# Attention and a gated MLP on one core: the scale of V from a reduction on GpSimd and powers of two on VectorE, in place of a transpose and spreading products on TensorE

## The chip, the core and the metric

The kernel runs on one core of a Trainium2 chip. A core has five engines, each with its own queue of instructions that it works through in order: TensorE (PE, matrix products), VectorE (DVE), ScalarE (ACT), GpSimd (POOL) and SyncE (SP, which issues the transfers here). They wait for each other through semaphores. The time is device microseconds of one execution; a kernel's figure is the median of several runs. One more execution of each kernel is recorded instruction by instruction; from it come the profile's page and the answers of the trace.

## The reference

Sliding-window attention with a linear bias, followed by a gated MLP that mixes along the sequence. B = 8 batches, H = 8 heads, S = 576 positions, D = 64, and d_model = 512, d_ff = 1024. All in 32-bit floats:

```python
scores = scale * np.matmul(q, k.transpose(0, 1, 3, 2))
mask = (rel >= 0) & (rel < window)                    # window = 128
scores = np.where(mask, scores + bias[None], -1e9)
attn = softmax(scores)
x = np.matmul(attn, v)                                # heads side by side: (B, S, 512)
h = np.maximum(x @ w_in, 0.0)
u, v = h[..., :512], h[..., 512:]
v_n = (v - mean(v)) / np.sqrt(var(v) + 1e-6)
v_s = np.einsum('ts,bsd->btd', w_spatial, v_n) + b_spatial[None, :, None]
return (u * v_s) @ w_out
```

## The kernel before

**Precision.** Every factor of a product is kept as two parts, a rounded one and the rest, and a product is made of three passes. In the attention of most pairs the two parts are 16-bit floats. For these, V has to be brought into the range of a 16-bit float first: it is multiplied with a power of two (`am[:, 5:6]`), split into `vh` and `vl`, and the result is multiplied with the inverse (`am[:, 6:7]`, which also takes out the factor 4096 of the probabilities).

**The work.** Heads are worked in pairs, `p` = 0 to 3, so there are 32 pairs of batch and heads. The first five (batch 0, and pair 0 of batch 1) go through `raw_tile`, which needs no scale. The other 27 go through `attention`: scores on PE (L520), bias, mask and minimum on VectorE (L531), exponentials and their sums on ScalarE (L537), the probabilities split into two 16-bit parts `pq` (L557 on ScalarE, L562 on VectorE), transposed by two transfers of SyncE into `pt` (L568), and multiplied with `vh` and `vl` on PE (L624). L633 and L637 scale the result back and split it into `xt`.

**The scale of V (L572 to L601),** once for each of the 27 pairs. ScalarE sums |V| along the free dimension (L579), which gives each of the 128 partitions one number, `am[:, 0:1]`. PE transposes this column into one row (L583), in a bank of PSUM that it takes from the ring `x` of two banks, the ring that the products L624 use as well. VectorE takes the maximum of the row and keeps it between two powers (L587, L588), in 16 bits. Two products of one column (L593) spread it back over 128 partitions, times 2^-12 and times 2^-13/4096 from the constant `ones`. VectorE keeps the exponents alone (L599) and turns the first into its inverse by an exclusive or (L600). Then V is scaled into `vh` (L604 on VectorE or L607 on ScalarE) and `vl` (L611).

**The gated part, `gated(b)`,** for each batch 29 units on PE, each into one of two banks `m`. First five v units, one for each block of positions (L689, and L711 for the last block of 64, which comes second): product, relu on ScalarE (L271), and the layer norm: statistics (L650 to L655, VectorE), 1/sqrt by a `pow` on GpSimd (L659), normalisation (L663, VectorE), then the split into `vn` (a copy by L267, and L700). The buffer `vt` of a block is one of two. Then come u units (L741, relu by L271 on ScalarE or L272 on VectorE), spatial units (L762, which need all five blocks of `vn`) and output units (L788): "uuuuusususs...", so five u units stand ahead of the first spatial one. GpSimd has little to do beside `pow`: constants at the start (L226 to L248, L386, L387), and two clearings of a part of `pq` ahead of the first scaled pair (L491).

**The order.** Nothing is ordered by hand. Each operation is added to a `Plan` with an engine (or a choice of two), a weight in ns, a due time, and what it reads and writes. `Plan.order` walks through time: whatever is ready, by its inputs and its ring of buffers, goes to its engine as soon as that is free, the earliest due time first, and holds the engine for its weight. The order that comes out is each engine's queue; on the chip the times are the chip's own and the order stays. The weights of the steps above: 95 for L583, 190 for L593, 400 for L587 and L588, 150 for L599 and L600, 550 for L659.

Of the kernel before, what the change touches and what calls it, by code (L numbers as in the profile page):

```python
# [9 lines left out]
F32 = mybir.dt.float32  # L10
F32R = mybir.dt.float32r
BF16 = mybir.dt.bfloat16
F16 = mybir.dt.float16
I32 = mybir.dt.int32
U32 = mybir.dt.uint32
AF = mybir.ActivationFunctionType
ALU = mybir.AluOpType
AX = mybir.AxisListType
# [120 lines left out]
def attn_gmlp_kernel(ctx, tc, qk, v, w_in, w_spT, b_sp, w_out, outT):  # L139
# [3 lines left out]
    nc = tc.nc  # L143
    B, H, D, _, S = qk.shape
    P = 2 * D
# [8 lines left out]
    PSC = 4096.0  # L154
    VORDER = (0, 4, 1, 2, 3)

    SWITCH = 190
# [12 lines left out]
    work = ctx.enter_context(tc.tile_pool(name="work", bufs=2))  # L170
    ps = ctx.enter_context(tc.tile_pool(name="ps", bufs=1, space=PSUM))
    ctx.enter_context(tc.manual_schedule())
    plan = Plan()

    def fixed(shape, dtype, name):
        t = const.tile(shape, dtype, name=name)
        return Buf(lambda: t)

    def dve(n, fast=False):
        return 75 + n / (1.92 if fast else 0.96)  # L180
# [13 lines left out]

    nhalf = fixed([P, 1], F32, "nhalf")
    ident = fixed([P, P], F32, "ident")
    ones = fixed([1, 2 * P], BF16, "ones")
    tabs = [fixed([P, 2 * P], BF16, f"tab{h}") for h in range(H)]
    win = fixed([P, NC_, 2, DF], F32R, "win")
    wout = fixed([P, ND, 2, DM], F32R, "wout")  # L200
# [10 lines left out]
    rstat = fixed([P, 8, 8], F32, "rstat")  # L211
# [12 lines left out]
    def constants():  # L224
        def f():
            nc.gpsimd.iota(relf(), [[-1, 2 * P]], base=P, channel_multiplier=1, allow_small_or_imprecise_dtypes=True)  # L226
        plan.add("POOL", 400, 0, f, (), [(relf, 0)])

        def f():
            nc.vector.memset(maskt(), 0.0)  # L230
        plan.add("DVE", dve(256), 0, f, (), [(maskt, 0)])

        def f():
            nc.gpsimd.affine_select(maskt(), maskt(), [[-1, 2 * P]], ALU.is_ge, MASKED, base=P, channel_multiplier=1)
            nc.gpsimd.affine_select(maskt(), maskt(), [[1, 2 * P]], ALU.is_ge, MASKED, base=-1, channel_multiplier=-1)
        plan.add("POOL", 800, 1, f, [(maskt, 0)], [(maskt, 0)])

        def f():
            nc.vector.memset(ident(), 1.0)
            nc.vector.memset(ones()[:, :P], 2.0 ** -12)  # L240
            nc.vector.memset(ones()[:, P:], 2.0 ** -13 / PSC)
            nc.vector.memset(nhalf(), -0.5)
            nc.vector.memset(rstat(), 1.0)
        plan.add("DVE", dve(400), 500, f, (), [(ident, 0), (ones, 0), (nhalf, 0)] + [(rstat, k) for k in range(8)])

        def f():
            nc.gpsimd.affine_select(ident(), ident(), [[-1, P]], ALU.is_ge, 0.0, base=0, channel_multiplier=1)
            nc.gpsimd.affine_select(ident(), ident(), [[1, P]], ALU.is_ge, 0.0, base=0, channel_multiplier=-1)  # L248
        plan.add("POOL", 600, 500, f, [(ident, 0)], [(ident, 0)])

        def f():
            nc.vector.tensor_scalar(minus(), ident(), -1.0, None, ALU.mult)
        plan.add("DVE", 150, 501, f, [(ident, 0)], [(minus, 0)])
        for j in range(2):
            def f(j=j):
                nc.vector.memset(stat[j](), 1.0)
            plan.add("DVE", dve(64), 600, f, (), [(stat[j], x) for x in range(99)])
        for h in range(H):
            def f(h=h):
                slope = 2.0 ** (-8.0 * (h + 1) / H)  # L260
                nc.vector.scalar_tensor_tensor(tabs[h](), relf(), -8.0 * slope, maskt(), ALU.mult, ALU.add)
            plan.add("DVE", dve(256), 1000 + h * 4000, f, [(relf, 0), (maskt, 0)], [(tabs[h], 0)])
# [237 lines left out]
    def attention(b, p):  # L500
# [11 lines left out]
        for g, banks in enumerate(PIECES):  # L512
            sc = [[plan.buf(ps, "s", 4, [P, 2, 2 * P], F32) for _ in range(2)] for _ in banks]
            span = [(k, i, t, min(P, S - t * P), max(0, (t - 1) * P), min(S, (t + 1) * P)) for k, ts_ in enumerate(banks) for i, t in enumerate(ts_)]

            def f(sc=sc, span=span):
                for k, i, t, m, k0, k1 in span:
                    for j in range(2):
                        rows = slice(j * D, (j + 1) * D)
                        nc.tensor.matmul(sc[k][j]()[:m, i, :k1 - k0], raw()[rows, 0, t * P:t * P + m], raw()[rows, 1, k0:k1],  # L520
                                         start=True, stop=True)
            plan.add("PE", SWITCH + pe(*[4 * (x[5] - x[4]) for x in span]), due - 5000 + g * 3000, f, RAWS,
                     [(sc[k][j], i) for k, i, *_ in span for j in range(2)])
            for k, i, t, m, k0, k1 in span:
                for j in range(2):
                    h, n, c0 = 2 * p + j, k1 - k0, P if t == 0 else 0
                    pt = lambda j=j, m=m, t=t, n=n: prob[j]()[:m, OFF[t]:OFF[t] + n]
                    d = due - 4500 + t * 700 + j * 200

                    def f(sc=sc[k][j], pt=pt, i=i, j=j, h=h, t=t, m=m, n=n, c0=c0):  # L530
                        nc.vector.tensor_tensor_reduce(pt(), sc()[:m, i, :n], tabs[h]()[:m, c0:c0 + n], -0.125, 3e38,  # L531
                                                       ALU.add, ALU.min, st()[:m, NM, j, t:t + 1])
                    cols = parts(prob[j], OFF[t], OFF[t] + n)
                    plan.add("DVE", dve(n), d, f, [(sc[k][j], i), (tabs[h], 0)], cols + [(st, (NM, j, t))])

                    def f(pt=pt, j=j, t=t, m=m):
                        nc.scalar.activation(pt(), pt(), AF.Exp, bias=st()[:m, NM, j, t:t + 1], scale=-1.0,  # L537
                                             accum_out=st()[:m, SM, j, t:t + 1])
                    plan.add("ACT", act(n, 2), d, f, cols + [(st, (NM, j, t))], cols + [(st, (SM, j, t))])
        pts = []  # L540
        for j in range(2):
            d = due + j * 1500
# [28 lines left out]

        vh, vl = (plan.buf(work, tag, 2, [P, NQ, P], F16) for tag in ("vh", "vl"))  # L572
        am = plan.buf(work, "am", 2, [P, 8], F32)
        one = plan.buf(work, "one", 2, [1, 2], BF16)
        mp = plan.buf(ps, "x", 2, [P, 512], F32)
        d = due - 3000

        def f():
# [1 line left out]
        plan.add("ACT", act(NQ * P, 1), d, f, VRS, [(vl, 0), (am, 0)])  # L580

        def f():
            nc.tensor.transpose(mp()[0:1, 0:P], am()[:, 0:1], ident())  # L583
        plan.add("PE", SWITCH // 2, d + 1, f, [(am, 0), (ident, 0)], [(mp, 0)])

        def f():
            nc.vector.tensor_reduce(one()[:, 0:1], mp()[0:1, 0:P], AX.X, ALU.max)  # L587
            nc.vector.tensor_scalar(one()[:, 0:1], one()[:, 0:1], 2.0 ** -98, 2.0 ** 126, ALU.max, ALU.min)  # L588
        plan.add("DVE", 400, d + 2, f, [(mp, 0)], [(one, 0)])

        def f():
            for k in range(2):
                nc.tensor.matmul(mp()[:, P + k:P + k + 1], ones()[:, k * P:(k + 1) * P], one()[:, 0:1], start=True, stop=True,  # L593
                                 skip_group_check=True)
        plan.add("PE", SWITCH, d + 3, f, [(one, 0), (ones, 0)], [(mp, 1)])

        def f():
            bits = 0x7F800000
            nc.vector.tensor_scalar(am()[:, 5:7].bitcast(I32), mp()[:, P:P + 2].bitcast(I32), bits, None, ALU.bitwise_and)  # L599
            nc.vector.tensor_scalar(am()[:, 5:6].bitcast(I32), am()[:, 5:6].bitcast(I32), bits, None, ALU.bitwise_xor)  # L600
        plan.add("DVE", 150, d + 4, f, [(mp, 1)], [(am, 1)])  # L601

        def fv():
            nc.vector.tensor_scalar(vh(), vr(), am()[:, 5:6], None, ALU.mult)  # L604
# [61 lines left out]
    def gated(b, xt, first=lambda t: None):  # L666
# [140 lines left out]
        for i, kind in enumerate(UORDER):  # L807
# [3 lines left out]
            {"u": u_unit, "s": sp_unit, "o": o_unit}[kind](*todo[kind].pop(0))  # L811

    constants()
    for c in range(NC_):
        win_weights(1, c, -30000 + 1000 * c, win_load(1, c, -30000 + 1000 * c, f"vn{c}", 1))
# [17 lines left out]
    for b in range(1, B):  # L833
        xt = []
        for p in range(NP):
            if b == 1 and (b, p) not in RAW and (b, p - 1) in RAW:
                clear()
            xt.append(attention(b, p))
        gated(b, xt)
# [33 lines left out]
```

## Time and profile before

| | us |
|---|---|
| median of 3 runs | 648.48 (648.08 to 651.25) |
| profiled execution, whole | 648.05 |
| its span in the trace | 646.3 |
| mean granted clock of TensorE | 0.992 |

Three timed runs and one profiled execution; the profiled one is 0.4 us below the median. Of the trace these groups belong to the scale of V (27 pairs):

| line, engine | count | busy, us | mean, ns |
|---|---|---|---|
| L579 ACT, sums of absolute values | 27 | 19.8 | 734 |
| L583 PE, transpose | 27 | 7.3 | 272 |
| L587 DVE, maximum | 27 | 7.4 | 273 |
| L593 PE, spreading | 54 | 5.3 | 165 |
| L599 DVE, exponents | 27 | 4.1 | 154 |
| L600 DVE, inverse | 27 | 4.2 | 154 |

A busy time counts the instruction's own duration, also where PE's pipeline lets neighbours overlap. A row of a group or of a timeline ends, where the engine was idle ahead of it, with how long and with what ended the idle time. "issue" is idle time without a wait that the profile shows. A time of a timeline is counted from the start of the span. Where an engine's name has a q behind it (POOLq), the row is of its sequencer, not of its arithmetic.

### The profile page before, as it was taken

The numbers are of one execution on the slowest core, as the hardware profiler recorded it, in microseconds if no ns is written. First come the engines' busy times: TensorE is split into PE (matmuls) and PEld (weight loads), VectorE is DVE, ScalarE is ACT, GpSimd is POOL, SyncE is SP. The second block draws the span as 40 slices with busy tenths as digits, with TensorE's granted clock in tenths as the row PEclk, the third lists the DMA queues.
The fourth block names the chain that finished last, engine by engine and source line by source line (L and its number), as shares of the span: only waits on it lengthen the run. The fifth ranks groups of instructions, "written<-read, shape, count | busy, mean of one in ns | idle before, by whom it ended". The sixth has DMA issues, their size and how long they took to land.

```text
span 646.3 us, 14141 instructions
## 1 busy us (share of the span) xinstructions
PE 619.0 (96%) x5037; PEld 529.8 (82%) x5037; DVE 524.2 (81%) x1897; ACT 430.9 (67%) x1322; POOL 29.6 (5%) x53
## 2 busy tenths in 40 slices
PE   4879999999999999999999999999999999999997
PEld 2445688778899879988898979988898978988997
DVE  6999898999887979887887979887887979873632
ACT  4698675989585848686686848676686857662211
POOL 1000010000200010000100010000100010000100
PEclk9998799999999999999999999999999999999999
DMA  7903013799156863778165753858166751733001
GB/s 264 329 20 130 19 62 119 169 209 202 55 132 133 190 107 93 155 155 184 40 143 127 191 112 89 154 152 188 32 154 125 193 113 10 132 79 76 2 20 55
DMA packets 149291, 79.34 MB, mean 123 GB/s; under 512 B 128610, under 2 KB 139874, under 8 KB 149220
## 3 DMA queue, kind: packets, MB, share of 16 engines
q1 hardware_dynamic: 149220, 78.44, 51.8%
q8 instruction: 39, 0.64, 0.4%
q14 instruction: 32, 0.26, 0.1%
HBM read 37.13 MB, written 9.44 MB: 72 GB/s over the span
## 4 chain that ended last, share of the span: by engine, by line
PE 79%; DVE 17%; issue 1%; DMA 1%; ACT 1%; SPq 1%; ACTq 0%; DVEq 0%
PE m L762 16%; PE m L741 16%; PE m L788 14%; PE m L689 13%; PE s L520 8%; PE x L624 6%; DVE pq L562 4%; PE m L711 2%; DVE prob L436 2%; DVE prob L531 2%; DVE gs L298 1%; DMA pt<-in_qk_dram 1%; DVE prob L450 1%; DVE u L770 1%; DVE o L267 1%
## 5 line engine op out<-in xcount | busy, mean ns | idle before, releaser
L537 ACT ACTIVATE prob<-prob,stat 128x128 f32<-128x128 f32 (+1 forms) x270 | 125.4, 466 | 13.6 <-DVE stat L531 12.4
L762 PE MATMUL m<-wsp,vn 128*128 128x288 f32 x768 | 124.3, 299 | 0.7 <-DVE u L770 0.7
L788 PE MATMUL m<-gs,wout 128*128 128x288 f32 x768 | 113.5, 301 | 0.3 <-DVE gs L776 0.2
L762 PEld LDWEIGHTS m<-wsp,vn 128*128 128x128 f32 x768 | 107.5, 188 | 6.7 <-issue 1.9
L557 ACT ACTIVATE pq<-prob,stat 128x128 f16<-128x128 f32 x270 | 103.1, 464 | 12.7 <-ACT prob L537 10.2
L741 PE MATMUL m<-xt,win 128*128 128x288 f32 x768 | 111.6, 298 | 0.0
L788 PEld LDWEIGHTS m<-gs,wout 128*128 128x128 f32 x768 | 103.3, 188 | 7.2 <-issue 1.7
L562 DVE SCALAR_TENSOR_TENSOR pq<-prob,stat,pq 128x128 f16<-128x128 f32 x270 | 104.0, 437 | 4.3 <-ACT pq L557 3.7
L741 PEld LDWEIGHTS m<-xt,win 128*128 128x128 f32 x768 | 103.9, 188 | 4.1 <-issue 2.3
L689 PE MATMUL m<-win,xt 128*128 128x512 f32 x384 | 93.5, 396 | 1.7 <-DVE o L267 1.7
L531 DVE CUSTOM_DVE_ANT_0 prob<-s,tab 128x128 f32<-128x128 f32 (+1 forms) x270 | 89.2, 376 | 2.6 <-PE s L520 2.1
L689 PEld LDWEIGHTS m<-win,xt 128*128 128x128 f32 x384 | 71.5, 189 | 18.2 <-DVE o L267 2.8
L520 PE MATMUL s<-qkraw 64*128 64x256 f32 (+2 forms) x540 | 66.5, 360 | 1.5 <-DVE stat L531 1.3
L770 DVE TENSOR_TENSOR u<-m,u 128x288 f32<-128x288 f32 x64 | 28.9, 451 | 34.2 <-PE m L762 34.2
L520 PEld LDWEIGHTS s<-qkraw 64*128 64x128 f32 (+1 forms) x540 | 42.0, 175 | 16.2 <-issue 9.0
L659 POOL TENSOR_TENSOR st<-st,nhalf 128x1 f32<-128x1 f32 (+1 forms) x40 | 25.6, 640 | 560.4 <-DVE st L655 548.0
L537 ACT ACTIVATION_READ_ACCUMULATOR prob<-prob,stat 128x1 f32 x270 | 50.6, 187 | 0.0
L267 ACT COPY o<-m 128x288 f32<-128x288 f32 x37 | 14.6, 395 | 46.2 <-PE m L788 45.9
L624 PE MATMUL x<-pt,vh 128*64 128x256 f16 (+6 forms) x756 | 41.7, 229 | 0.0
L271 ACT ACTIVATE vt<-m 128x512 f32<-128x512 f32 x31 | 18.5, 598 | 33.0 <-DVE st L654 16.1
L637 DVE SCALAR_TENSOR_TENSOR xt<-x,am,xt 128x288 fp32r<-128x288 f32 x54 | 26.2, 507 | 17.1 <-ACT xt L633 17.0
L624 PEld LDWEIGHTS <-vh 128*64 128x64 f16 x756 | 31.7, 110 | 5.8 <-issue 3.5
(132 smaller groups left out, 820.7 us busy)
## 6 DMA issues: line engine op xcount, KB each, us to landing
qkraw<-in_qk_dram SPq DMA_DIRECT2D x28, 576.0 KB, 3.9
out_dram<-o SPq DMA_DIRECT2D x64, 144.0 KB, 2.0
vraw<-in_v_dram SPq DMA_DIRECT2D x28, 320.0 KB, 2.9
vn<-in_w_in_dram SPq DMA_DIRECT2D x6, 512.0 KB, 7.1
pt<-in_w_out_dram SPq DMA_DIRECT2D x4, 512.0 KB, 4.5
gs<-in_w_spT_dram SPq DMA_DIRECT2D x4, 288.0 KB, 5.0
xt<-in_w_in_dram SPq DMA_DIRECT2D x2, 512.0 KB, 6.8
qkraw<-in_qk_dram SPq DMA_DIRECT2D x3, 320.0 KB, 8.3
```

The lines of the kernel that those rows point to most:

```text
L520: nc.tensor.matmul(sc[k][j]()[:m, i, :k1 - k0], raw()[rows, 0, t * P:t * P + m], raw()[rows, 1, k0:k1], start=True, stop=True)
L531: nc.vector.tensor_tensor_reduce(pt(), sc()[:m, i, :n], tabs[h]()[:m, c0:c0 + n], -0.125, 3e38, ALU.add, ALU.min, st()[:m, NM, j, t:t + 1])
L537: nc.scalar.activation(pt(), pt(), AF.Exp, bias=st()[:m, NM, j, t:t + 1], scale=-1.0, accum_out=st()[:m, SM, j, t:t + 1])
L557: nc.scalar.activation(pq[j]()[:m, 0, cs], prob[j]()[:m, cs], AF.Copy, scale=st()[:m, RC, j, t:t + 1])
L562: nc.vector.scalar_tensor_tensor(pq[j]()[:m, 1, cs], prob[j]()[:m, cs], st()[:m, RC, j, t:t + 1], pq[j]()[:m, 0, cs], ALU.mult, ALU.subtract)
L624: nc.tensor.matmul(xp()[j * D:(j + 1) * D, x0:x0 + n], l()[:, kt, j * D:(j + 1) * D], rhs[:, o:o + n], start=j not in seen, stop=False, sk ...
L637: nc.vector.scalar_tensor_tensor(xt()[:, S + R + hf * HS:S + R + (hf + 1) * HS], xp()[:, :HS], am()[:, 6:7], xt()[:, qs].bitcast(F32), ALU ...
L689: nc.tensor.matmul(pt(), xt[c]()[:, X0[a] + t * P:X0[a] + (t + 1) * P], win()[:, c, w, DH:DF], start=(n == 0), stop=(n == 3 * NC_ - 1))
L741: nc.tensor.matmul(pt()[:, :HS], win()[:, c, w, d * P:(d + 1) * P], xt[c]()[:, X0[a] + hf * HS:X0[a] + (hf + 1) * HS], start=(n == 0), sto ...
L762: nc.tensor.matmul(pt()[:, :HS], l, r, start=(n == 0), stop=(n == len(ops) - 1))
L770: nc.vector.tensor_tensor(u(), pt()[:, :HS], u(), ALU.mult)
L788: nc.tensor.matmul(pt()[:, :HS], wout()[:, d, w, e * P:(e + 1) * P], gs[d]()[:, a, :], start=(n == 0), stop=(n == 3 * ND - 1))
```

## The change

The column `am[:, 0:1]` no longer goes to PE. GpSimd takes the maximum over the 128 partitions and gives it to all of them (`partition_all_reduce`, weight 4000 in the plan). VectorE then limits it, keeps the exponent, multiplies it with the two powers of two, now a constant of 128 partitions by two columns (`powers`), and inverts the first: four operations. `one`, the bank `mp` of the ring `x` and the constant `ones` go. The maximum is no longer rounded to 16 bits on its way; only its exponent is used, as before.

```diff
-    ones = fixed([1, 2 * P], BF16, "ones")
+    powers = fixed([P, 2], F32, "powers")
...
-            nc.vector.memset(ones()[:, :P], 2.0 ** -12)
-            nc.vector.memset(ones()[:, P:], 2.0 ** -13 / PSC)
+            nc.vector.memset(powers()[:, 0:1], 2.0 ** -12)
+            nc.vector.memset(powers()[:, 1:2], 2.0 ** -13 / PSC)
...
-        one = plan.buf(work, "one", 2, [1, 2], BF16)
-        mp = plan.buf(ps, "x", 2, [P, 512], F32)
...
         def f():
-            nc.tensor.transpose(mp()[0:1, 0:P], am()[:, 0:1], ident())
-        plan.add("PE", SWITCH // 2, d + 1, f, [(am, 0), (ident, 0)], [(mp, 0)])
-
-        def f():
-            nc.vector.tensor_reduce(one()[:, 0:1], mp()[0:1, 0:P], AX.X, ALU.max)
-            nc.vector.tensor_scalar(one()[:, 0:1], one()[:, 0:1], 2.0 ** -98, 2.0 ** 126, ALU.max, ALU.min)
-        plan.add("DVE", 400, d + 2, f, [(mp, 0)], [(one, 0)])
-
-        def f():
-            for k in range(2):
-                nc.tensor.matmul(mp()[:, P + k:P + k + 1], ones()[:, k * P:(k + 1) * P], one()[:, 0:1], start=True, stop=True,
-                                 skip_group_check=True)
-        plan.add("PE", SWITCH, d + 3, f, [(one, 0), (ones, 0)], [(mp, 1)])
+            nc.gpsimd.partition_all_reduce(am()[:, 1:2], am()[:, 0:1], P, bass.bass_isa.ReduceOp.max)
+        plan.add("POOL", 4000, d + 1, f, [(am, 0)], [(am, 2)])
 
         def f():
             bits = 0x7F800000
-            nc.vector.tensor_scalar(am()[:, 5:7].bitcast(I32), mp()[:, P:P + 2].bitcast(I32), bits, None, ALU.bitwise_and)
+            nc.vector.tensor_scalar(am()[:, 2:3], am()[:, 1:2], 2.0 ** -98, 2.0 ** 126, ALU.max, ALU.min)
+            nc.vector.tensor_scalar(am()[:, 2:3].bitcast(I32), am()[:, 2:3].bitcast(I32), bits, None, ALU.bitwise_and)
+            nc.vector.tensor_scalar(am()[:, 5:7], powers(), am()[:, 2:3], None, ALU.mult)
             nc.vector.tensor_scalar(am()[:, 5:6].bitcast(I32), am()[:, 5:6].bitcast(I32), bits, None, ALU.bitwise_xor)
-        plan.add("DVE", 150, d + 4, f, [(mp, 1)], [(am, 1)])
+        plan.add("DVE", 400, d + 4, f, [(am, 2), (powers, 0)], [(am, 1)])
```

More of the change, by code (lines that the diff above doesn't have):

```diff
@@ L239, in f @@
             nc.vector.memset(ident(), 1.0)
-            nc.vector.memset(ones()[:, :P], 2.0 ** -12)
-            nc.vector.memset(ones()[:, P:], 2.0 ** -13 / PSC)
+            nc.vector.memset(powers()[:, 0:1], 2.0 ** -12)
+            nc.vector.memset(powers()[:, 1:2], 2.0 ** -13 / PSC)
             nc.vector.memset(nhalf(), -0.5)
             nc.vector.memset(rstat(), 1.0)
-        plan.add("DVE", dve(400), 500, f, (), [(ident, 0), (ones, 0), (nhalf, 0)] + [(rstat, k) for k in range(8)])
+        plan.add("DVE", dve(400), 500, f, (), [(ident, 0), (powers, 0), (nhalf, 0)] + [(rstat, k) for k in range(8)])
         def f():
```

## The prediction

> **What bounds the kernel now.** I read the page of the profile first: the span, then the busy times of the engines.
>
> ```profile
> span 646.3 us, 14141 instructions
> PE 619.0 (96%) x5037; PEld 529.8 (82%) x5037; DVE 524.2 (81%) x1897; ACT 430.9 (67%) x1322; POOL 29.6 (5%) x53
> PE 79%; DVE 17%; issue 1%; DMA 1%; ACT 1%; SPq 1%; ACTq 0%; DVEq 0%
> ```
>
> TensorE (PE) is busy for 96% of the span and makes up 79% of the chain that ended last. So a microsecond taken out of PE's queue is nearly a microsecond of the time, and a microsecond in which PE starves is lost. GpSimd (POOL) is idle 95% of the time, which looks like free room. But what matters is who stands behind GpSimd in the stage in which the new instruction falls. That stage is seen in the timelines of GpSimd, ScalarE (ACT), VectorE (DVE) and PE around the layer norms of batch 4. First GpSimd, whose rows here are the five `pow` (L659), and the first `pow` of batch 5:
>
> ```profile
> 381.76 0.54 POOL L659 TENSOR_TENSOR st<-st,nhalf 64x1 f32<-64x1 f32 x1 [2.64 <-DVE st L655]
> 384.81 0.98 POOL L659 TENSOR_TENSOR st<-st,nhalf 128x1 f32<-128x1 f32 x1 [2.51 <-DVE st L655]
> 388.17 0.55 POOL L659 TENSOR_TENSOR st<-st,nhalf 128x1 f32<-128x1 f32 x1 [2.38 <-DVE st L655]
> 390.04 0.55 POOL L659 TENSOR_TENSOR st<-st,nhalf 128x1 f32<-128x1 f32 x1 [1.32 <-DVE st L655]
> 451.53 0.55 POOL L659 TENSOR_TENSOR st<-st,nhalf 128x1 f32<-128x1 f32 x1 [60.94 <-DVE st L655]
> ```
>
> The columns are the start, the duration, engine and line, and the idle time before with what ended it. Then ScalarE: the sums of |V| (L579), whose result `am` the new reduction reads, the copy of a normalised row block (`vn`) and the relu of the first u unit:
>
> ```profile
> 384.97 0.19 ACT L579 ACTIVATION_READ_ACCUMULATOR vl<-vraw 128x1 f32 x1
> 389.65 0.62 ACT L267 CAST vn<-vt 128x512 fp32r<-128x512 f32 x1 [1.21 <-DVE vt L663]
> 391.45 0.39 ACT L271 ACTIVATE u<-m 128x288 f32<-128x288 f32 x1
> 445.99 0.19 ACT L579 ACTIVATION_READ_ACCUMULATOR vl<-vraw 128x1 f32 x1
> ```
>
> And the first and the last of six such sums that lie among a batch's five `pow` (batches 1 to 6), with the `pow` of that moment:
>
> ```profile
> 168.01 0.73 ACT L579 ACTIVATE vl<-vraw 128x640 f16<-128x640 f32 x1
> 168.59 0.98 POOL L659 TENSOR_TENSOR st<-st,nhalf 128x1 f32<-128x1 f32 x1 [2.77 <-DVE st L655]
> 530.26 0.73 ACT L579 ACTIVATE vl<-vraw 128x640 f16<-128x640 f32 x1
> 530.74 0.98 POOL L659 TENSOR_TENSOR st<-st,nhalf 128x1 f32<-128x1 f32 x1 [2.51 <-DVE st L655]
> ```
>
> **Where the reduction falls.** The planner gives GpSimd whatever is ready when it is free. `am` is complete at 384.97+0.19 = 385.16 us, while the third `pow` runs (384.81 to 385.79); the fourth isn't ready before 388.17. So the reduction is put between the third and the fourth `pow`. It is the same in all six batches from 168.01 to 530.26 us; batches 0 and 7 have no sum inside. Another reduction always comes some 5 us ahead of a batch's first `pow`: the sums end at 445.99+0.19 = 446.18, `pow` starts at 451.53, a gap of 5.35 us. The other two of the four per batch lie tens of microseconds from any `pow`.
>
> **What it removes.** On PE one transpose (L583) and two products of one column (L593) for each of 27 pairs. Their view by line:
>
> ```profile
>   issue: 7.0, 27
>   DVE one L588: 0.9, 1
>   DVE am L599: 12.3, 12
> L587 DVE TENSOR_REDUCE one<-x x27: 269/273/277, 111.4 to 572.2; 1x1 bf16<-1x128 f32 x27
> L588 DVE TENSOR_SCALAR one<-one x27: 144/144/146, 111.7 to 572.5; 1x1 bf16<-1x1 bf16 x27
> L599 DVE TENSOR_SCALAR am<-x x27: 139/159/160, 112.8 to 574.3; 128x2 int32<-128x2 int32 x27
> L600 DVE TENSOR_SCALAR am<-am x27: 153/153/155, 113.0 to 574.5; 128x1 int32<-128x1 int32 x27
> ```
>
> PE sat idle 7.0 us ahead of the weight loads of L593 (27 times 0.26) and 0.9 us for L588; all of it goes: 7.9 us. The transposes I leave out: PE starts a matmul 0.03 us after L583 in the rows below (391.12, 391.15). The 12.3 us are VectorE waiting for L593; they go too, but in a stage bound by PE they bring nothing of their own (between 0 and 12.3; I take 0). VectorE's own work stays: out go 0.273+0.144+0.159+0.153 = 0.73 us for each pair, in come four operations on one or two columns, priced by L600 at 4 x 0.153 = 0.61 us. With the bank of PSUM for L583 gone, a pair's scale is known long before its products; they then wait for the transposed `pt`, as now, so nothing is won there.
>
> **What it adds: the turn on GpSimd.** The reduction is no operation of the trace. Bounds for one word per partition: 0.34 us (the iota below) to 0.98 (the long `pow` at 384.81); I take the usual `pow`, 0.55. More matters what it may bring along:
>
> ```profile
> L226 POOLq MODIFY_POOL_CONFIG  x2: 11/11/11, 0.8 to 0.8; - x2
> L226 POOL IOTA u<- x1: 344/344/344, 0.9 to 0.9; 128x256 f32 x1
> ```
>
> The program set up GpSimd's configuration once, ahead of its first iota, and for nothing else: iota and `pow` are served by one set of code. A custom operation over partitions is not among the kinds seen, and I hold it likeliest that it needs another set. Then each turn from `pow` to reduction or back fetches code, and the fetch holds GpSimd's queue. The pair here cost nothing (iota follows at once), so the trace shows the switch but not its price when the code is not there. [...]
>
> [...]
>
> ```profile
> q8 instruction: 39, 0.64, 0.4%
> xt<-in_w_in_dram SPq DMA_DIRECT2D x2, 512.0 KB, 6.8
> qkraw<-in_qk_dram SPq DMA_DIRECT2D x3, 320.0 KB, 8.3
> ```
>
> The instruction queue took 0.4% of 16 engines' span, 41 us, for 39 packets: 1.1 us each. [...]
>
> **What stands behind it.** VectorE runs in order: L663, which needs the `pow`, holds all VectorE work behind it, and ScalarE, in order too, holds the relu of the first u unit behind its copy of `vn`:
>
> ```profile
> 389.08 0.53 DVE L663 TENSOR_SCALAR vt<-vt,st 128x512 f32<-128x512 f32 x1
> 391.12 0.27 PE L583 MATMUL x<-ident,am 128*1 128x128 f32 x1
> 391.15 1.84 PE L741 MATMUL m<-xt,win 128*128 128x288 f32 x12
> 392.92 0.54 PE L520 MATMUL s<-qkraw 64*64 64x192 f32 x4
> 393.53 5.04 PE L741 MATMUL m<-xt,win 128*128 128x288 f32 x36
> 398.41 0.56 PE L762 MATMUL m<-wsp,vn 128*128 128x288 f32 x3
> ```
>
> PE has two banks `m`. Without them evacuated it can do the second u unit and the small L520 and then stands before the third u unit, 393.53 us. With GpSimd taken for X after 385.79, the fourth `pow` ends X+0.55 later, then come L663 (0.53), the copy (0.62) and the relu (0.39): PE can go on at 387.88+X. So the cover is 393.53-387.88 = 5.65 us; a reduction alone (0.55) is hidden, two fetches are not. X = 6.8+0.55+6.8 = 14.15, the loss 14.15-5.65 = 8.5 us. The first spatial product (398.41) moves by the same, since the five u units stand before it.
>
> At the head of the batch only the fetch back is in the way, since the one towards the reduction runs in idle time: 0.55+6.8 against the gap of 5.35 is 2.0 us. It shifts all five `pow` (each row block needs a buffer `vt` that the block two before frees) and so adds to the above: 10.5 us a batch, six batches, 63.0 us.
>
> Once, ahead of the first scaled pair, the reduction also stands among the two clearings of `pq`:
>
> ```profile
> 108.17 0.99 POOL L491 MEMSET pq<- 128x512 f16 x2 [15.02 <-PE x L476]
> L604 DVE TENSOR_SCALAR vh<-vraw,am x19: 539/553/554, 113.3 to 574.7; 128x640 f16<-128x640 f32 x19
> ```
>
> With a fetch after the first clearing (108.7) the scale is known at 108.7+6.8+0.55+0.61 = 116.7 instead of 113.3. That is 3.4 us late on VectorE, between 0 and 3.4 for PE; I take 3.
>
> **The sum.** The profiled execution took 648.05 us, 1.75 more than its span; the median of the three timed runs is 648.48, 0.4 above it. 648.05 + 63.0 + 3.0 - 7.9 = 706.2 us. With a fetch of 5.0 us a batch loses 4.9+0.2 and the time is 674; with 8.3 it loses 11.5+3.5 and the time is 733, with the same one-time 3 us.
>
> **The rivals.**
>
> One: no code is fetched, the two kinds share a set. For it speaks that the one configuration in the trace cost nothing and that four kinds ran on it; against it, that the new kind is none of these. Then X is 0.55, even a reduction of 4 us (the weight in the diff) stays under the cover of 5.65, and only the removal is left: 648.05-7.9 = 640.2 us, faster. The point that decides is X = 5.65 us, a fetch of 2.55. Chance 0.12.
>
> Two: fetches, but the shorter way to the scale moves the reduction out of the five `pow`, ahead of the first or behind the last. The margin is small (`am` complete 0.6 us before the third `pow` ends, 3.0 before the fourth starts), but the sums wait for buffers that the products of an earlier pair free, and these stay where they are. Then a batch loses only the 2.0 us at its head: 648.05+12.0+3.0-7.9 = 655 us. Chance 0.08.
>
> Three: the stall hits PE harder than by the u units. VectorE falls behind by all of the `pow`'s delay, (385.79+14.15+0.55) - (388.17+0.55) = 11.8 us, and at 81% busy it makes up little before it feeds the products of the attention behind. With the 2.0 that is 13.8 us a batch: 648.05+82.8+3.0-7.9 = 726 us. Chance 0.20.
>
> **How the numbers follow.** The forecast, fetches between the `pow`, has 0.58, and I give 706 us; what is left, 0.02, is for ways not named. The forecast's own range is 674 to 733 by the price of a fetch. The range for 8 in 10 takes in the second rival below and, above, the third with a dearer fetch, 745; it leaves out the first rival. A change of 0.5% (3.2 us) is about what a measurement of this kernel can tell from none. Faster: the first rival, 0.12. Slower: the forecast and rivals two and three, nearly all of the 0.86, less the case that prices come out near the cover: 0.84. Same: 0.04.
>
> **What would show it.** Right: configuration instructions of GpSimd in many places instead of one; the third and fourth `pow` of batches 1 to 6 some 15 us apart instead of 3.4, with the reduction between them; VectorE's idle time before L663 with GpSimd as releaser, some 50 us in total instead of next to none; PE idle before L741 and digits under 9 once a batch in PE's row of slices; the waits at L593 gone. Wrong: reductions and `pow` alternating at under 1 us, or no reduction between the `pow`.

## The result, and the profile after

The changed kernel takes 708.14 us (704.84 to 709.12, four runs) against 649.44 us for the kernel before in its four runs (648.08 to 651.25): 1.0893 times as long, 95% interval 1.0844 to 1.0942. The profiled execution took 709.12 us, of which the trace spans 707.3. The forecast was 706.

First the page: the span, the busy times, the chain that ended last, and two groups of PE's with the idle time ahead of them. L751 is the spatial product (L762 before), L678 the v unit (L689 before).

```profile
span 707.3 us, 14062 instructions
PE 627.2 (89%) x4956; PEld 543.3 (77%) x4956; DVE 530.8 (75%) x1906; ACT 427.9 (61%) x1313; POOL 40.0 (6%) x80
PE 53%; DVE 26%; issue 10%; ACT 4%; DMA 2%; POOL 2%; SPq 1%; POOLq 0%; ACTq 0%; DVEq 0%
L751 PE MATMUL m<-wsp,vn 128*128 128x288 f32 x768 | 129.3, 309 | 33.7 <-ACT u L271 33.7
L678 PE MATMUL m<-win,xt 128*128 128x512 f32 x384 | 94.8, 400 | 9.2 <-ACT vt L271 8.1
```

PE, VectorE and ScalarE have about the same work as before, but PE now stands for 707.3-627.2 = 80.1 us of the span, where it stood for 27.3. Its part of the chain is down from 79% to 53%, and 10% of the chain is "issue", time for which the profile shows no wait. GpSimd (POOL) is busy for only 40 us, so its share of busy time says nothing about what it costs. 33.7 us of PE's idle time stand ahead of the first spatial product of five batches.

Then GpSimd's own rows, by the lines of the two kinds: L581 is the reduction, L648 the `pow` (L659 before).

```profile
L581 POOL PARTITION_ALL_REDUCE am<-am x27: 350/375/630, 115.5 to 624.0; - x27
L581 POOLq MODIFY_POOL_CONFIG  x26: 1/3/22, 109.8 to 604.2; - x26
L648 POOLq MODIFY_POOL_CONFIG  x26: 82/83/83, 164.3 to 624.6; - x26
DVE vt L652 <- POOL st L648: 60.2, 12, 7.6
```

The configuration instruction, which stood once (as a pair) ahead of the first iota, now stands ahead of 13 reductions and of 13 `pow`, in pairs: 26 changes of configuration. Both its halves last under 0.1 us in these rows. What it costs is seen only in the idle time behind it. And the last row, from the view of who waited for whom, gives the victim: VectorE waited 60.2 us, 12 times, for a `pow`.

The page's row of the instruction queue is the same as before, 39 packets:

```profile
q8 instruction: 39, 0.64, 0.4%
```

So no row shows code being moved; that code is loaded is the forecast's reading alone. "Fetch" below is the name for the hold of GpSimd's queue behind a configuration instruction, and kinds of work that follow each other without one are said to share a "set of code".

One batch in time, GpSimd (start, duration, and the idle time before):

```profile
411.15 0.35 POOL L581 PARTITION_ALL_REDUCE am<-am  x1 [20.46 <-ACT vl L577]
418.45 1.20 POOL L648 TENSOR_TENSOR st<-st,nhalf 128x1 f32<-128x1 f32 x2 [6.95 <-issue]
424.03 0.55 POOL L648 TENSOR_TENSOR st<-st,nhalf 128x1 f32<-128x1 f32 x1 [4.37 <-DVE st L644]
425.11 0.72 POOL L648 TENSOR_TENSOR st<-st,nhalf 128x1 f32<-128x1 f32 x1 [0.53 <-DVE st L644]
431.71 0.38 POOL L581 PARTITION_ALL_REDUCE am<-am  x1 [5.89 <-DVE stat L531]
438.91 0.59 POOL L648 TENSOR_TENSOR st<-st,nhalf 128x1 f32<-128x1 f32 x1 [6.82 <-issue]
```

Here a fetch is to be read in brackets: 5.89 us from the fourth `pow` to the reduction, 6.82 from the reduction to the fifth `pow`. The second is put down to "issue", since its inputs had long been there. The first is put down to whoever came last among the reduction's inputs, which is misleading: the sums that it needs ended at 427.3. Over the trace the way to the reduction, where its inputs are there, takes 5.6 to 6.2 us and the way back 6.7 to 7.8. At the head of the batch (418.45) the fetch back makes the first two `pow` come together.

And what stood behind it, from the timelines of VectorE, ScalarE and PE:

```profile
439.53 0.55 DVE L652 TENSOR_SCALAR vt<-vt,st 128x512 f32<-128x512 f32 x1 [6.62 <-POOL st L648]
440.11 0.62 ACT L267 CAST vn<-vt 128x512 fp32r<-128x512 f32 x1 [7.15 <-DVE vt L652]
442.60 0.39 ACT L271 ACTIVATE u<-m 128x288 f32<-128x288 f32 x1
435.21 1.79 PE L520 MATMUL s<-qkraw 64*128 64x128 f32 x16
443.04 1.09 PE L751 MATMUL m<-wsp,vn 128*128 128x288 f32 x3 [6.04 <-ACT u L271]
```

It is the chain of the forecast: `pow`, normalisation, copy, relu of a u unit, and PE before its bank. Three products of L751 take 1.09 us behind the stall where they took 0.56 before. The windows view (length, busy times with counts, then PE's granted clock, 0.50, 0.50 and 1.00) has the clock beside it:

```profile
444.00:446.00 2.00, 2.00 (x10) 2.00 (x10) 1.86 (x10) 1.95 (x6) 0.00 (x0) 0.50 0.47 90
446.00:447.00 1.00, 1.00 (x6) 1.00 (x5) 1.00 (x4) 0.77 (x4) 0.00 (x0) 0.50 1.18 217
450.00:455.00 5.00, 5.00 (x42) 4.40 (x42) 3.91 (x16) 4.93 (x18) 0.00 (x0) 1.00 0.59 163
```

After the stall PE's granted clock is 0.50 until about 447.7 us, 4.7 us behind the start of the first product, and 1.00 from there. Batch 1 is the exception: there the reduction lies behind the third `pow`, and PE stands ahead of the score products instead:

```profile
192.96 2.35 PE L520 MATMUL s<-qkraw 64*128 64x256 f32 x8 [6.51 <-DVE stat L531]
```

### The profile page after: what moved, and what is told of

Its sections match the earlier page's. It is cut to its first block, busy times and chain, and to the rows that moved or that the text cites. A ratio compares the mean times of both kernels' runs of the same rounds, so it can differ in the third digit from the quotient of the medians.

```text
span 707.3 us, 14062 instructions
## 1 busy us (share of the span) xinstructions
PE 627.2 (89%) x4956; PEld 543.3 (77%) x4956; DVE 530.8 (75%) x1906; ACT 427.9 (61%) x1313; POOL 40.0 (6%) x80
## 4 chain that ended last, share of the span: by engine, by line
PE 53%; DVE 26%; issue 10%; ACT 4%; DMA 2%; POOL 2%; SPq 1%; POOLq 0%; ACTq 0%; DVEq 0%
PE m L751 16%; PE m L777 14%; PE m L730 8%; PE s L520 4%; DVE pq L562 4%; PE x L613 4%; PE m L678 3%; DVE st L639 3%; DVE prob L531 2%; ACT prob L537 2%; DVE vn L689 2%; DVE vt L652 1%; POOL st L648 1%; ACT pq L557 1%; DVE prob L436 1%
## 5 line engine op out<-in xcount | busy, mean ns | idle before, releaser
L751 PE MATMUL m<-wsp,vn 128*128 128x288 f32 x768 | 129.3, 309 | 33.7 <-ACT u L271 33.7
L751 PEld LDWEIGHTS m<-wsp,vn 128*128 128x128 f32 x768 | 114.0, 199 | 38.6 <-ACT u L271 35.7
L777 PE MATMUL m<-gs,wout 128*128 128x288 f32 x768 | 115.9, 305 | 0.0
L777 PEld LDWEIGHTS m<-gs,wout 128*128 128x128 f32 x768 | 106.2, 193 | 8.3 <-issue 2.5
L730 PEld LDWEIGHTS m<-xt,win 128*128 128x128 f32 x768 | 107.4, 193 | 5.4 <-ACT vt L271 2.8
L678 PE MATMUL m<-win,xt 128*128 128x512 f32 x384 | 94.8, 400 | 9.2 <-ACT vt L271 8.1
L678 PEld LDWEIGHTS m<-win,xt 128*128 128x128 f32 x384 | 72.7, 192 | 26.1 <-ACT vt L271 8.6
L520 PE MATMUL s<-qkraw 64*128 64x256 f32 (+2 forms) x540 | 69.9, 373 | 16.3 <-DVE stat L531 16.3
L520 PEld LDWEIGHTS s<-qkraw 64*128 64x128 f32 (+1 forms) x540 | 44.4, 182 | 31.3 <-DVE stat L531 20.7
L652 DVE TENSOR_SCALAR vt<-vt,st 128x512 f32<-128x512 f32 (+1 forms) x40 | 21.6, 541 | 60.7 <-POOL st L648 60.2
L267 ACT CAST vn<-vt 128x512 fp32r<-128x512 f32 x27 | 16.6, 616 | 62.6 <-DVE vt L652 62.6
L648 POOL TENSOR_TENSOR st<-st,nhalf 128x1 f32<-128x1 f32 (+1 forms) x40 | 24.7, 619 | 242.4 <-DVE st L644 142.6
```

The costliest lines, as they stand in the source:

```text
L267: plan.either([("ACT", act(n), lambda: nc.scalar.copy(*ap())), ("DVE", dve(n, fast), lambda: nc.vector.tensor_copy(*ap()))], due, reads, w ...
L648: nc.gpsimd.tensor_tensor(st()[:m, 11:12], st()[:m, 10:11], nhalf()[:m], ALU.pow)
L678: nc.tensor.matmul(pt(), xt[c]()[:, X0[a] + t * P:X0[a] + (t + 1) * P], win()[:, c, w, DH:DF], start=(n == 0), stop=(n == 3 * NC_ - 1))
L730: nc.tensor.matmul(pt()[:, :HS], win()[:, c, w, d * P:(d + 1) * P], xt[c]()[:, X0[a] + hf * HS:X0[a] + (hf + 1) * HS], start=(n == 0), sto ...
L751: nc.tensor.matmul(pt()[:, :HS], l, r, start=(n == 0), stop=(n == len(ops) - 1))
L777: nc.tensor.matmul(pt()[:, :HS], wout()[:, d, w, e * P:(e + 1) * P], gs[d]()[:, a, :], start=(n == 0), stop=(n == 3 * ND - 1))
```

## The experiments

The theory: changes of configuration between `pow` and reduction, 13 each way, are the loss. They hold GpSimd's queue for 5.6 to 7.8 us each, VectorE and ScalarE stand in order behind it, and PE behind those. Rivals: the order that the plan makes of a weight of 4000 (A), the reduction or the waits for its result (B), the new steps on VectorE (C). A question of its own is the granted clock of 0.50 (D). The kernel before ran on the same chip beside each group, at 650.1 to 650.3 us.

**One code set, all else the same.** The queues stay in the changed kernel's order. `affine_select` stands in the place of `pow` and copies the variance, so this kernel leaves out the reciprocal square root.

```diff
-            nc.gpsimd.tensor_tensor(st()[:m, 11:12], st()[:m, 10:11], nhalf()[:m], ALU.pow)
+            nc.gpsimd.affine_select(st()[:m, 11:12], st()[:m, 10:11], [[0, 1]], ALU.is_ge, 0.0, base=0, channel_multiplier=1)
```

> The changed kernel, with the pow of the layer norm replaced by an affine_select that copies the variance: the reciprocal square root is left out, the order of all queues and every wait for GpSimd stay, with the reduction among the layer norms. If affine_select is served by the same code as the reduction, no fetch is left after the first. Theory: 638 to 648 us. Rivals A and B: 690 to 710, since order and reductions are the same.

645.70 us, 0.9931 times the kernel before (0.9913 to 0.9949). GpSimd in the same stage, and the page's line:

```profile
393.89 0.37 POOL L648 TENSOR_SCALAR_AFFINE_SELECT st<-st 128x1 f32<-128x1 f32 x1 [0.90 <-DVE st L644]
396.18 0.35 POOL L581 PARTITION_ALL_REDUCE am<-am  x1 [1.92 <-DVE vn L689]
398.77 0.18 POOL L648 TENSOR_SCALAR_AFFINE_SELECT st<-st 128x1 f32<-128x1 f32 x1 [2.24 <-DVE st L644]
PE 610.5 (95%) x4956; PEld 529.5 (82%) x4956; DVE 528.8 (82%) x1906; ACT 425.9 (66%) x1313; POOL 24.7 (4%) x80
```

The reduction stands at the same place, between the fourth and the fifth block, and no engine waits for it (of all 27 reductions only the first is waited for, 1.7 us by VectorE). That rules out A and B as the main cause: the same order, the same 27 reductions, 62 us less. It also splits the loss. Of the 707.3-644.4 = 62.9 us between the two spans, PE's idle time makes up (707.3-627.2)-(644.4-610.5) = 46.2, and its busy time, in the same 4956 products, 627.2-610.5 = 16.7: those products ran slower. This kernel has a standstill of its own at its start (below), so 62.9 is rather too little for what the changes of configuration cost.

One thing in it was not foreseen: GpSimd stands 7.98 us ahead of the first iota, where it stood 0.65 in the changed kernel.

```profile
8.48 0.34 POOL L226 IOTA u<- 128x256 f32 x1 [7.98 <-issue]
```

No run shows the cause.

**The way to the scale without the gain.** The reduction is added to the kernel before, with no reader.

```diff
+        def f():
+            nc.gpsimd.partition_all_reduce(am()[:, 1:2], am()[:, 0:1], P, bass.bass_isa.ReduceOp.max)
+        plan.add("POOL", 4000, d + 1, f, [(am, 0)], [(am, 2)])
+
         def f():
             nc.tensor.transpose(mp()[0:1, 0:P], am()[:, 0:1], ident())
```

> The kernel before, with a reduction added at the place that the change gives it (weight 4000) and its result unused: transpose, spreading products and their waits all stay. Theory: the loss is GpSimd's turn alone, so all of it comes, and the 7.9 us that the removal saved are missing: 708 + 8 = 716 us, 708 to 724. Rival C (it is the new way to the scale, the four operations and their waits on VectorE, that costs): 648 to 655.

727.43 us, 1.1196 times (1.1147 to 1.1244). The loss needs neither the new steps on VectorE nor a reader of the result, so C is out as its cause. It came 3 us over the range that I gave. In this kernel the reduction lies where the forecast had put it, behind the third `pow`:

```profile
425.97 0.99 POOL L663 TENSOR_TENSOR st<-st,nhalf 128x1 f32<-128x1 f32 x1 [2.57 <-DVE st L659]
432.84 0.38 POOL L583 PARTITION_ALL_REDUCE am<-am  x1 [5.88 <-ACT u L271]
440.87 1.21 POOL L663 TENSOR_TENSOR st<-st,nhalf 128x1 f32<-128x1 f32 x2 [7.66 <-issue]
```

The last two `pow` come together behind it, so two blocks of the layer norm are late, not one. The size can't be carried over to the changed kernel, because most of the stall reaches PE by another way here, the old way to the scale: VectorE's maximum stands behind the late normalisation, and PE, in order, stands before the spreading products (L597):

```profile
PE x L597 <- DVE one L592: 44.5, 6, 9.4
```

**The plan's weight.** `plan.add("POOL", 400, ...)` in place of 4000.

> The changed kernel with the plan's weight of the reduction at 400 in place of 4000; the reductions still lie among the pow, with as many fetches. Theory: 700 to 715 us. Rival A: under 690, since the plan no longer delays the pow behind the reduction.

732.87 us, 1.1287 times (1.1250 to 1.1324): outside both expectations, on the far side. The weight matters, but the other way round. With 400 the reduction lies behind the third `pow` in most batches, and PE is stopped twice:

```profile
444.12 3.25 PE L730 MATMUL m<-xt,win 128*128 128x288 f32 x12 [5.43 <-ACT vt L271]
452.20 3.25 PE L730 MATMUL m<-xt,win 128*128 128x288 f32 x12 [4.83 <-ACT u L271]
452.00:457.00 5.00, 4.80 (x22) 3.98 (x24) 4.17 (x21) 4.41 (x17) 0.61 (x1) 0.51 0.00 0
```

Both stalls together are 10.3 us, and twelve products of a u unit take 3.25 us at half the clock (the last row, 0.51) where they took 1.84. So the 4000 of the diff helped: it moved the reduction one `pow` further back, where all five u units were still to be had as cover.

**Twice the fetches.** Each reduction is followed by a `pow` of its own and by the reduction again.

```diff
+            nc.gpsimd.partition_all_reduce(am()[:, 3:4], am()[:, 0:1], P, bass.bass_isa.ReduceOp.max)
+            nc.gpsimd.tensor_tensor(am()[:, 4:5], am()[:, 3:4], nhalf(), ALU.pow)
             nc.gpsimd.partition_all_reduce(am()[:, 1:2], am()[:, 0:1], P, bass.bass_isa.ReduceOp.max)
```

> The changed kernel, with each reduction followed by a pow of its own and the reduction again: two fetches more for each pair, 1.4 us more of work. Theory: among the pow two fetches more, some 13 us, and as much at the head of a batch, six times each: 708 + 160 = 868 us, 840 to 890. Rival B: 1.4 us a pair, some of it hidden: 708 to 745.

1019.6 us, from a single execution: far above both. 54 more fetches cost 1019.6-708.1 = 311 us, 5.8 us each, nearly their whole length (GpSimd's waits ahead of the added instructions come to 351 us, 6.5 each). I had counted only those around the layer norms and taken the ones of the other pairs for hidden. They aren't:

```profile
DVE am L588 <- POOL am L583: 294.1, 27, 16.0
```

VectorE waits for the reduction in all 27 pairs, since its steps stand in its queue where the plan expected the result. GpSimd's idle time did not hide these fetches, because VectorE's queue already stood at their result.

**Putting the reductions behind the last `pow`.** `last_pow[0]` is set in `layer_norm` to the result of the latest `pow`. First pair 2 alone, the one that lies among the `pow`; then pairs 1 and 2, so that the one ahead of the first `pow` goes too (`p in (1, 2)`).

```diff
+        behind = [last_pow[0]] if b > 1 and p in (2,) else []
-        plan.add("POOL", 4000, d + 1, f, [(am, 0)], [(am, 2)])
+        plan.add("POOL", 4000, d + 1, f, [(am, 0)] + behind, [(am, 2)])
```

> The changed kernel, with only the reduction of pair 2 put behind the last pow (the one that lies among the pow); the one some 5 us ahead of the first pow stays. Theory: the stall of 6 to 7 us in six batches goes, the fetch back at the head stays, at 1.5 to 3.5 us a batch: 650 to 668 us, between the kernel with both behind and the changed one. Rivals A and B: over 690.

657.04 us, 1.0115 times (1.0086 to 1.0145): as expected. 51 of the 59 us that the change lost are gone, with the same number of reductions and the plan's weight untouched. The move also gathers the changes of configuration: this kernel has 14 in place of 26, and so have the next two.

> The changed kernel, with the reductions of pairs 1 and 2 of batch b+1 put behind the last pow of batch b, so that a batch has one fetch of code each way and both lie in GpSimd's idle stretches. Theory (fetches between pow and reduction are the loss): the six stalls ahead of the spatial units and the waits at the head of the batches go, only the one-time 3 us stays: 640 to 648 us. Rival A (the order that the plan makes of a weight of 4000 is worse): still over 690. Rival B (the reduction itself, or VectorE waiting for it, costs): still over 680, since there are as many reductions.

661.52 us, 1.0193 times (1.0164 to 1.0221): wrong, by 13 us, and slower than with one of them moved. Who waited for the reduction, in the kernel with both behind:

```profile
  DVE am L589: 16.0, 7
```

Seven waits of 2.3 us on VectorE. The fetch towards the reduction now runs right behind the last `pow`, and VectorE's steps come 4 us behind it by the plan, before the fetch is over. So the next kernel tells the plan: 9000 for the first reduction behind the `pow`, 500 for the others.

> The kernel with both reductions behind the last pow, and the plan's weights made true: 9000 for the first reduction behind the pow, which has a fetch ahead of it, 500 for the others (4000 each so far). Theory: what was left there (661 in place of 640 to 648) is VectorE standing before the scale steps while the fetch towards the reduction runs, because the plan put them too early; with the right weights 640 to 650 us. Rival (putting off the scale of two pairs delays their products): still 658 or more.

645.97 us, 0.9942 times (0.9924 to 0.9960). The row in this kernel:

```profile
  DVE am L589: 6.0, 1
```

One wait is left, at the first scaled pair. The change as it was meant, with the same 27 reductions and 14 changes of configuration in place of 26, is faster than the kernel before by 0.6%, since hardly any queue stands behind a fetch. It does not beat the next one.

**Half of the change, in the code of `pow`.** GpSimd's `tensor_reduce` over the partitions; the spreading products stay on PE.

```diff
-            nc.tensor.transpose(mp()[0:1, 0:P], am()[:, 0:1], ident())
-        plan.add("PE", SWITCH // 2, d + 1, f, [(am, 0), (ident, 0)], [(mp, 0)])
+            nc.gpsimd.tensor_reduce(am()[0:1, 1:2], am()[:, 0:1], AX.C, ALU.max)
+        plan.add("POOL", 4000, d + 1, f, [(am, 0)], [(am, 2)])
...
-            nc.vector.tensor_reduce(one()[:, 0:1], mp()[0:1, 0:P], AX.X, ALU.max)
-            nc.vector.tensor_scalar(one()[:, 0:1], one()[:, 0:1], 2.0 ** -98, 2.0 ** 126, ALU.max, ALU.min)
-        plan.add("DVE", 400, d + 2, f, [(mp, 0)], [(one, 0)])
+            nc.vector.tensor_scalar(one()[:, 0:1], am()[0:1, 1:2], 2.0 ** -98, 2.0 ** 126, ALU.max, ALU.min)
+        plan.add("DVE", 150, d + 2, f, [(am, 2)], [(one, 0)])
```

> Half of the change: the maximum over partitions on GpSimd by tensor_reduce, which gives one number on one partition, and the spreading products on PE as before. If that instruction is served by the same code as pow, no fetch comes. Theory: 643 to 652 us. Rival B (work over partitions on GpSimd among the pow costs, whatever its code): 680 or more.

640.19 us, 0.9848 times (0.9810 to 0.9886), the fastest of all here, faster than both kernels, and 3 us below the range that I gave. GpSimd takes turns between the two kinds without any configuration instruction:

```profile
384.38 1.06 POOL L658 TENSOR_TENSOR st<-st,nhalf 128x1 f32<-128x1 f32 x2 [4.20 <-DVE st L653]
390.30 0.55 POOL L658 TENSOR_TENSOR st<-st,nhalf 128x1 f32<-128x1 f32 x1 [4.85 <-DVE st L654]
392.53 0.46 POOL L583 CROSS_LANE_REDUCE am<-am 128x1 f32<-128x1 f32 x1 [1.68 <-ACT vl L579]
PE 611.8 (96%) x5010; PEld 530.4 (83%) x5010; DVE 523.2 (82%) x1890; ACT 421.7 (66%) x1302; POOL 48.2 (8%) x80
```

The last line is the page's and is used further below. The maximum over partitions took 0.46 us of GpSimd in these rows; in the changed kernel a fetch took 5.6 to 7.8. With the plan's weight at 500:

> The kernel with the maximum by tensor_reduce in the code of pow, with the plan's weight at 500 in place of 4000. Theory: nothing waits for GpSimd in either, so 637 to 643 us, the same as with 4000.

640.71 us, 0.9873 times (0.9840 to 0.9905): the same, as expected.

**PE kept busy in the stall.** The score products ahead of it are issued four times over.

```diff
-            def f(sc=sc, span=span):
-                for k, i, t, m, k0, k1 in span:
+            def f(sc=sc, span=span, again=4 if g == 0 and p == 2 and b > 2 else 1):
+                for k, i, t, m, k0, k1 in span * again:
```

> The changed kernel, with the 16 score products that stand last in PE's queue ahead of the stall issued four times over (same inputs, same results) in five of the six batches, so that PE is busy through most of the stall. The waits stay what they are. Theory D (after the stall TensorE runs at half its clock for some 7 us, and that costs some 3 us a batch): the clock after the stall is 1.0 and the time falls by 8 to 16 us, to 692 to 700. Rival (the lower clock is only a mark of the idle time and costs nothing): 706 to 712, since the added products fill idle time only.

701.04 us (ratio to the kernel before 1.0798, 1.0762 to 1.0834): 7 us faster than the changed kernel, with 240 products more. That is 1 us short of the range for theory D, and 5 us below that of its rival. PE's rows at the same place, and the window with the clock behind the stall:

```profile
431.47 6.34 PE L520 MATMUL s<-qkraw 64*128 64x128 f32 x64
439.11 0.67 PE L751 MATMUL m<-wsp,vn 128*128 128x288 f32 x3 [1.29 <-ACT u L271]
440.00:442.00 2.00, 2.00 (x18) 2.00 (x17) 1.86 (x9) 1.88 (x6) 0.00 (x0) 1.00 0.44 88
```

The wait for the relu is still there, filled with products that nobody needs, and the clock behind it is 1.00. So in this kernel the lower clock is a price and not only a mark. Its size is less sure. In the two traces the spans differ by 8.0 us, but 2.4 of these are fetches that happened to be shorter here (the five pairs behind the fourth `pow` come to 64.6 us, in the changed kernel to 67.0), and 1.4 lie ahead of batch 1's first `pow`. That leaves about 4 us, 0.8 for each of the five stalls. Not all of the clock is regained by this: its mean is 0.970 in this profiled execution, 0.949 in the changed kernel's and 0.984 in that of the kernel without fetches. The stall of batch 1, 6.51 us in the changed kernel with a clock of 0.50 until about 198.5 us, is not among the five.

## Why the prediction was right

**The mechanism** is shown, but for what the configuration does while GpSimd is held: fetches at each change between `pow` and reduction (no fetch, no loss, with the same queues), through VectorE's and ScalarE's order, onto PE's banks `m`. Rival one (no fetch) falls with the 26 changes of configuration. Its arithmetic has a use all the same: the kernel with the maximum in `pow`'s code came to the 640 us that the rival gave for a change without fetches, though by other terms (below). Rival two (no reduction among the `pow`) is what the kernel with pair 2 put behind made true: 657 us where it gave 655.

**The price of a fetch** was well sized: 6.8 taken, 5.6 to 6.2 towards and 6.7 to 7.8 back measured, 12.7 for the pair in the rows above (5.89+6.82) in place of 13.6. That the 6.8 fits so well is luck: it was my estimate from the landing of a 512 KB load of weights, and no run shows that a change of configuration moves anything, or how much. The runs showed the holds themselves in its place. The 5.0 and 8.3 of the forecast's range are shown by no run as prices either, and the instruction queue has 39 packets before and after.

**The place** failed: "the reduction is put between the third and the fourth `pow`". In batches 2 to 6 it lies between the fourth and the fifth; only in batch 1 did the forecast's place come true. I read it off the timeline of before, but the plan is made anew with the weight of 4000. In the rows above GpSimd was taken for X = 438.91-425.83 = 13.1 us and PE stood 6.0, so the cover there was 7.0 us, not 5.65. In the five batches the stall was 6.0 to 7.3 us, not 8.5. Where the reduction does lie behind the third `pow` (weight 400), the kernel took 732.9 us, nearer to rival three's 726 than to 706: at that place the loss per batch was under-sized, since two blocks come late and PE stops twice. That the forecast's 706 was met with the reduction at another place is luck.

**The clock** was missing from the sum. Of the 62.9 us between the changed kernel and the one without fetches 46.2 are standstill, and 16.7, a quarter, are slower products. Term by term: the sum had 6 x 8.5 = 51.0 us for the stalls and 6 x 2.0 = 12.0 for the heads of the batches, and PE's own waits are 33.7+6.5 = 40.2 and 8.1 (ahead of L678, in the lines at the top). Both terms were over-sized, and the missing one about filled the gap to the 66.6 us that the fetches cost in all (below).

**The removal** was under-sized. From the first `pow` of batch 1 to the end, before and in three kernels:

```profile
162.33 0.55 POOL L659 TENSOR_TENSOR st<-st,nhalf 128x1 f32<-128x1 f32 x1 [53.17 <-DVE st L655]
```

```profile
171.62 0.59 POOL L648 TENSOR_TENSOR st<-st,nhalf 128x1 f32<-128x1 f32 x1 [7.25 <-DVE vt L709]
```

```profile
175.31 0.43 POOL L648 TENSOR_SCALAR_AFFINE_SELECT st<-st 128x1 f32<-128x1 f32 x1 [5.37 <-DVE st L644]
```

```profile
164.11 0.56 POOL L658 TENSOR_TENSOR st<-st,nhalf 128x1 f32<-128x1 f32 x1 [2.76 <-DVE st L654]
```

These are the kernel before, the changed one, the one with one code set, and the one with the maximum in `pow`'s code. Taken from their spans (646.3, 707.3, 644.4, 639.2) they leave 484.0, 535.7, 469.1 and 475.1 us. So without fetches the change saves 14.9 us here, not 7.9, and the transposes that I left out ("the transposes I leave out") make up about 8.9 of it: the kernel that drops them alone, with the spreading products kept, is that much shorter. PE's busy time there is 619.0-611.8 = 7.2 us below that of the kernel before, nearly all of the 7.3 us that the 27 transposes have as durations. I had read one instance, 0.03 us to the next matmul, as if the transpose cost PE nothing. The bank that the transposes take from the ring `x` goes with them too. The plan's order differs as well, so the 8.9 aren't the transposes' own time alone; and in the kernel with one code set the instruction in `pow`'s place is shorter than `pow` (0.18 to 0.43 us in these rows against 0.55 to 0.98), which may have a share in the 14.9. The fetches cost 535.7-469.1 = 66.6 us in this stretch, where the sum had 63.0.

**Up to the first `pow` of batch 1** the changed kernel lost 171.62-162.33 = 9.3 us, where the one-time term had 3 (and batch 1's head 2.0, counted among the 63.0).

So the sum of 58 came close to the measured 61 of the spans in part by luck, with errors that offset each other: the fetches at 63.0 for 66.6, the removal at 7.9 for 14.9, the start at 3 for 9.3, and inside the 66.6 a smaller stall than forecast and a clock that wasn't forecast. The sign and the rough size rest on the mechanism; that the forecast came within 2 us doesn't.

## What to carry to other kernels

GpSimd, busy for 6% of the span here, made a kernel 59 us slower, since the engines that waited for it had other work behind the wait in their queues: price a new instruction by how long its queue is held, from the row of the wait behind it, not by its busy time. On GpSimd look for the configuration instruction between different kinds of work (26 of its pairs between `pow` and reduction went with 708 us, none between `pow` and maximum with 640), keep to kinds that the trace shows without one in between, or gather the others in one stretch and give the plan the true time until their result (646 us). And price a stall of PE with the products behind it: here they came at a granted clock of 0.50 for 3.0 to 4.7 us.

## What the runs showed of the hardware that was not expected

- In the changed kernel a change of GpSimd's configuration held its queue for 5.6 to 6.2 us towards the reduction, where its inputs were there, and 6.7 to 7.8 back to `pow`, and the configuration instruction itself shows as under 0.1 us. Iota and `pow` ran with no change between them in the kernel before, `pow` and the maximum by `tensor_reduce` in the kernel with that maximum, 640 us. In the kernel with one code set `affine_select` (0.18 to 0.43 us) started 1.70 and 2.24 us behind a reduction, without a hold. In the changed kernel `affine_select` also ran at 2.66 us, behind the iota, and the clearing ran both at 109.37, ahead of the first reduction, and at 115.77, between two of them.
- After stalls of 6.0 to 7.3 us in the changed kernel TensorE's granted clock was 0.50 until 3.0 to 4.7 us after the products had begun again, in five stalls (443.0 to 447.7 is the longest). PE's products took 16.7 us more in all than in the kernel with one code set. The kernel that issued products that nothing reads through the stalls was 7 us faster, of which its trace puts about 4 down to the clock.
- The maximum of one column over 128 partitions took 0.35 to 0.63 us as the all-reduce in the changed kernel and 0.22 to 1.69 us as `tensor_reduce` in the kernel of 640 us.
